# A two-layer MoE behind attention on one core: first layer's activation applied in place to batches of whole chunks, evictions as plain copies

## The chip, the cores and the metric

One core of a Trainium2 chip. The time is device microseconds of one execution of the whole program. The kernel before ran three times: median 517.15 us, 516.41 to 517.77 us.

## The reference

Local attention plus attention on a four-fold downsampled sequence, for 2 batches x 8 heads x 576 positions x 64; its result is x, 1152 tokens x 512. Then two layers of matmuls in float32 accuracy:

```python
h = x @ w_in                                   # 1152x512 @ 512x2048
sp = np.where(h > 20.0, h, np.log1p(np.exp(np.minimum(h, 20.0))))
g = h * np.tanh(sp)                            # Mish
x = g @ w_out                                  # 2048 -> 512
silu = (x @ w_gate) * sigmoid(x @ w_gate)      # 512 -> 1536
out = (silu * (x @ w_val)) @ w_out2            # 1536 -> 512
```

The weights come as 64-bit floats.

## The kernel before

**Work.** Everything stays on chip between the stages. Float32 accuracy is made from pairs: each operand is split into a rounded part (`hi`, a copy to another type) and the rest (`lo`, a subtraction), and three matmuls (`mm3`, lines 763 to 765) take the place of one. A weight strip of 128 x 512 is loaded as raw 64-bit words and rebuilt by `convert`: two ScalarE steps with the function Prelu (`fold`, line 286; `field`, line 290), a VectorE step (`join`, line 293), then `hi` (line 219 on ScalarE or 221 on VectorE) and `lo` (line 307).

**First layer.** `l1(f, i)` makes chunk f (128 of the 2048 hidden columns, 16 chunks) for piece i of the tokens (three pieces of 384): a group of 12 matmuls in two halves (`cols_group`) into one of seven PSUM banks. The bank is emptied into a third of the chunk's H buffer. For chunks 0 to 5 and pieces 0 and 1 that is a plain copy (`early`), since the attention still runs; in all other cases the activation Mish is applied on the way (line 803, ScalarE). `split` then applies Mish in place to the two copied pieces of chunks 0 to 5 (line 822), and splits the whole chunk of 1152 tokens into G (`hi`, line 219 or 221; `lo`, line 829). There are six H and six G buffers; chunk 6 takes the H buffer of chunk 0, and so on. `l2` multiplies G with the second weight, four chunks at a time, in twelve groups of 12 matmuls. The second layer (`l3`, `l4`) follows, with Silu on ScalarE.

**Order.** A planner (`Plan.run`) writes the order of every engine before anything is issued. Each step has the engines that may run it with a cost on each, its dependencies, the buffers that it takes, and a due time `want`; among the steps that could start, an engine takes the one with the least `want`. ScalarE's functions come in tables: a step may name a table, and when this is not the last one loaded, the planner adds 8.0 to its due time and 1.28 us to its cost. Mish names "mish", the exponentials of the attention "exp", Silu "silu"; `fold` and `field` name none. Where nothing is ready, PE gets a filler matmul (`warm`, line 1194, the first 95 us only), so that it is never idle for long. Each engine then works through its order and waits where an input is not there.

In the names of the rows: b is a PSUM bank, H a chunk, G its split, cw a weight under conversion, raw its bytes, wt its split, xy the tokens' split x, warm the filler's bank.

Of the kernel before, what the change touches and what calls it, by code (L numbers as in the profile page):

```python
# [22 lines left out]
NTOK = 1152  # L23
PC = 384
# [8 lines left out]


SLOPE = 2.0 ** -40


class Ring:
# [37 lines left out]
class Plan:  # L76
# [15 lines left out]
    def run(self):  # L92
        names = ["PE", "ACT", "DVE", "POOL", "SP"]
        free = dict.fromkeys(names, 0.0)
        ready = {e: [] for e in names}
        for n, o in enumerate(self.ops):
            o.n = n
            if not o.left:
                for e in o.eng:
                    ready[e].append(o)  # L100
        table, now, order = None, 0.0, []
        todo = len(self.ops)
        while todo:
            later, ran = [], False
            for e in names:
                if free[e] > now:
                    later.append(free[e])
                    continue
                best = None
                for o in ready[e]:  # L110
                    t = o.at
                    for r in o.rings:
                        t = max(t, r.free_at(sum(x.ring is r for x in o.new)))
                    if t > now:
                        later.append(t)
                        continue
                    w = o.want + (8.0 if o.table and o.table != table else 0.0)
                    if best is None or (w, o.n) < best[0]:
                        best = ((w, o.n), o)
                if best is None:  # L120
                    if e == "PE" and self.spare and self.spare[1] <= now < self.spare[2]:
                        free[e] = now + self.spare[3] * (2 if now < COLD else 1)
                        later.append(free[e])
                        order.append((now, self.spare[0], e))
                        ran = True
                    continue
                o = best[1]
                ran = True
                todo -= 1
                for f in o.eng:  # L130
                    ready[f].remove(o)
                for x in o.new:
                    x.ring.give(x)
                d = o.eng[e]
                if o.table and o.table != table:
                    d, table = d + self.TABLE, o.table
                free[e] = now + (d if e != "SP" else max(0.5, d))
                o.ran = e
                o.end = free[e] + (2.2 if e == "SP" else 0.0)
                later.append(free[e])  # L140
                order.append((now, o, e))
                for x in o.use:
                    x.left -= 1
                    x.free_at = max(x.free_at, o.end + self.REMOTE)
                for c in o.out:
                    c.left -= 1
                    same = e in c.eng and len(c.eng) == 1
                    c.at = max(c.at, free[e] if same and e in ("PE", "SP") else o.end + (self.LOCAL if same else self.REMOTE))
                    if not c.left:
                        for f in c.eng:  # L150
                            ready[f].append(c)
            if not ran:
                nxt = [t for t in later if now < t < 1e8]
                if not nxt:
                    raise RuntimeError("no order found: " + str([(o.fn.__qualname__.split(".")[-1], [next((t for t, r in self.rings.items() if r is x.ring), "?") for x in o.new], o.at) for e in names for o in ready[e]]))
                now = min(nxt)
        self.length = max(o.end for o in self.ops)
        for _, o, e in order:
            o.fn(e)
# [3 lines left out]
def attention_moe_kernel(  # L163
# [38 lines left out]
    def us_tt(n):  # L202
        return n / 960 + 0.069
# [4 lines left out]
    def us_act(n, psum=False):  # L208
        return n / 1200 + (0.051 if psum else 0.093)
# [48 lines left out]
    def convert(kind, f, want, lead=None):  # L258


        src = srcs[kind]
        wide = src.dtype != F32
        m = 8 if wide else 1
        src = src.bitcast(U8) if wide else src
        raw = buf(wp, [128, 4104 if wide else 512], U8 if wide else F32, "raw", RAWS)
        wt = buf(wp, [128, 2, 512], F32R, "wt", WTS)
        cw = buf(wp, [128, 512], F32, "cw", CWS) if wide else raw
        w0 = want - (lead or 10.33)

        def load(e):  # L270
            t = raw.make()
            t = t[:, 1:4097] if wide else t
            if kind in "1gv":
                nc.sync.dma_start(
                    out=t.rearrange("p (c f) -> p c f", c=4),
                    in_=src[:, 128 * m * f:128 * m * (f + 1)].rearrange("(c p) f -> p c f", p=128),
                )
            else:
                nc.sync.dma_start(out=t, in_=src[128 * f:128 * (f + 1), :])

        prev = conv_chain[0] or {}
        o_load = plan.add({E_SP: 1.46}, load, [prev.get("load")], w0 - 10.0, [raw])
        last = o_load
        if wide:
            def fold(e):
                ACT.activation(cw.make(), raw.tile[:, 8:4104].bitcast(I8).rearrange("p (n b) -> p n b", b=8)[:, :, 0],  # L286
                               AF.Prelu, scale=-1.0, bias=-56.0, alpha=SLOPE)

            def field(e):
                ACT.activation(cw.tile.bitcast(I32), cw.tile, AF.Prelu, scale=-2.0 ** 27 / SLOPE, bias=-112 * 2.0 ** 27, alpha=SLOPE)  # L290

            def join(e):
                DVE.scalar_tensor_tensor(out=cw.tile.bitcast(U32), in0=raw.tile[:, 0:4096].bitcast(U32).rearrange("p (n b) -> p n b", b=2)[:, :, 1],  # L293
                                         scalar=5, in1=cw.tile.bitcast(U32), op0=ALU.logical_shift_right, op1=ALU.bitwise_or)

            o_mag = o = plan.add({"ACT": us_act(512) + 0.1}, fold, [o_load, prev.get("mag")], w0, [cw], [raw])
            o = plan.add({"ACT": us_act(512)}, field, [o], w0, use=[cw])
            last = plan.add({"DVE": us_tt(512)}, join, [o], w0 + 1, use=[cw, raw])
        else:
            o_mag = None  # L300

        def hi(e):
            wt.make()
            copy(e, wt.tile[:, 0], cw.tile)

        def lo(e):
            DVE.tensor_tensor(out=wt.tile[:, 1], in0=cw.tile, in1=wt.tile[:, 0].bitcast(F32), op=ALU.subtract)  # L307

        o_hi = plan.add({"ACT": us_act(512), "DVE": us_ts(512)}, hi, [last, prev.get("hi")], w0 + 2, [wt], [cw])
        o_lo = plan.add({"DVE": us_tt(512)}, lo, [o_hi], w0 + 3, use=[wt, cw])  # L310
        conv_chain[0] = {"load": o_load, "mag": o_mag, "hi": o_hi}
        wts[kind, f], wt_ops[kind, f] = wt, o_lo
        return cw, last
# [473 lines left out]
    def l1(f, i, want):  # L787
# [6 lines left out]
        first = h.first is None  # L794
        ps, o, cs = cols_group("1", f, i, lambda: xt, xd + [h.first], want, [x_buf] + ([] if first else [h]), [h] if first else [])

        early = f < RING and i < 2

        def evac(e):
            if early:  # L800
                copy(e, h.tile[:, cs], ps.tile[:, 0:n])
            else:
                ACT.activation(h.tile[:, cs], ps.tile[:, 0:n], AF.Mish)  # L803

        if early:
            o = plan.add({"ACT": us_act(n, True), "DVE": us_tt(n)}, evac, [o], want - 4, use=[ps, h])
        else:
            o = plan.add({"ACT": us_act(n, True)}, evac, [o] + att_ops, want - 4, use=[ps, h], table="mish")
        if first:
            h.first = o  # L810
        h.ops.append(o)
        if i == 2:
            split(f, h, want)

    def split(f, h, want):

        add = plan.add
        g = G[f] = buf("g", GSHAPE, F32R, "G", 6)
        n = 2 * PC

        def mish(e):
            ACT.activation(h.tile[:, 0:n], h.tile[:, 0:n], AF.Mish)

        def hi(e):
            g.make()
            copy(e, g.tile[:, 0], h.tile)

        def lo(e):
            DVE.tensor_tensor(out=g.tile[:, 1], in0=h.tile, in1=g.tile[:, 0].bitcast(F32), op=ALU.subtract)

        if f < RING:
            h.ops.append(add({"ACT": us_act(n)}, mish, h.ops[:2] + att_ops, want - 2, use=[h], table="mish"))
        o = add({"ACT": us_act(NTOK), "DVE": us_ts(NTOK)}, hi, h.ops + att_ops, want + 4.0, [g], [h])
        G_ops[f] = add({"DVE": us_tt(NTOK)}, lo, [o], want + 4.0, use=[g, h])

    yacc = buf("acc", [128, 4, NTOK], F32, "acc", 1)
# [392 lines left out]
```

## Time and profile before

| | us |
|---|---|
| median of three runs | 517.15 |
| profiled execution, its own time | 517.0 |
| its span | 515.2 |
| PE busy | 494.1 |
| ACT busy | 339.0 |
| DVE busy | 323.2 |
| ACT table loads, 58 of 1283 ns | 74.4 |

PE is TensorE, ACT ScalarE, DVE VectorE. The time is 1.8 us above the span, which begins with the first and ends with the last recorded instruction. A busy share is a mean over stages; where an engine sets the pace is seen in the view by stretches and in the list of waits. A matmul's row lasts longer (some 0.34 us) than its distance to the next (0.17 us), since matmuls are pipelined.

### The profile page before, as it was taken

The page shows a single profiled execution, that of the slowest core. Times are in us where ns is not written, and L with a number is a line of the kernel's source. Part 1 is how long each engine was busy: PE and PEld are TensorE (multiplying, and loading weights), DVE is VectorE, ACT ScalarE, POOL GpSimd, SP SyncE. Part 2 cuts the span into 40 slices and gives each one's busy share as a digit, 9 for nine tenths or more (in the row PEclk, how much of TensorE's full clock was granted, in tenths as well). Part 3 has the DMA queues.
Part 4 walks back from the last instruction along what each step waited for, and adds up shares of the span by engine and source line. Part 5 has one row for each costly group of instructions (what it writes and reads, how often), then busy time and mean ns, then how long its engine had stood idle before and what let it go on. Part 6 is the DMA issues. An engine that isn't in the chain of part 4 may idle for free.

```text
span 515.2 us, 8535 instructions
## 1 busy us (share of the span) xinstructions
PE 494.1 (96%) x3315; PEld 459.3 (89%) x3315; DVE 323.2 (63%) x624; ACT 339.0 (66%) x681; POOL 23.9 (5%) x43
## 2 busy tenths in 40 slices
PE   9999999999669996999999999999999999999997
PEld 7777888999559986999999999999998899998885
DVE  3897999744421523563458899989886088882422
ACT  4889999899995999369925376655573276750000
POOL 4332210000000000000000000000000000000000
PEclk9999999999989999999999999999999999999999
DMA  9999734322231132212321113242254014320022
GB/s 175 194 159 219 183 108 133 124 83 81 71 91 44 42 122 83 83 41 83 122 83 42 41 41 124 83 122 83 82 164 124 0 42 123 93 72 1 0 91 93
DMA packets 58225, 48.23 MB, mean 94 GB/s; under 512 B 30664, under 2 KB 53448, under 8 KB 58184
## 3 DMA queue, kind: packets, MB, share of 16 engines
q1 hardware_dynamic: 58184, 47.68, 34.7%
q8 instruction: 26, 0.43, 0.4%
q14 instruction: 15, 0.12, 0.1%
HBM read 45.31 MB, written 2.36 MB: 93 GB/s over the span
## 4 chain that ended last, share of the span: by engine, by line
PE 75%; ACT 19%; issue 3%; DVE 2%; DMA 1%; ACTq 0%
PE b L763 17%; PE b L765 17%; PE b L764 17%; PE b L1051 5%; PE b L1053 5%; PE b L1052 5%; ACT L803 3%; PE warm L1194 2%; ACT L290 2%; ACT cw L286 2%; ACT L286 2%; ACT H L803 2%; PE b L643 2%; ACT cw L290 1%; PE b L698 1%
## 5 line engine op out<-in xcount | busy, mean ns | idle before, releaser
L763 PE MATMUL b<-xy,wt 128*128 128x384 f32 x384 | 129.9, 338 | 3.7 <-ACT H L803 3.7
L765 PE MATMUL b<-xy,wt 128*128 128x384 f32 x384 | 128.6, 335 | 0.0
L764 PE MATMUL b<-xy,wt 128*128 128x384 f32 x384 | 128.6, 335 | 0.0
L293 DVE SCALAR_TENSOR_TENSOR cw<-raw,cw 128x512 uint32<-128x512 uint32 x68 | 46.6, 687 | 64.3 <-ACT cw L290 64.2
L763 PE MATMUL b<-G,wt 128*128 128x384 f32 x192 | 66.2, 345 | 11.1 <-ACT H L803 10.5
L763 PEld LDWEIGHTS b<-xy,wt 128*128 128x128 f32 x384 | 72.1, 188 | 5.3 <-ACT H L803 4.7
L764 PEld LDWEIGHTS b<-xy,wt 128*128 128x128 f32 x384 | 72.1, 188 | 0.0
L765 PEld LDWEIGHTS b<-xy,wt 128*128 128x128 f32 x384 | 72.1, 188 | 0.0
L765 PE MATMUL b<-G,wt 128*128 128x384 f32 x192 | 65.1, 339 | 0.0
L764 PE MATMUL b<-G,wt 128*128 128x384 f32 x192 | 65.0, 338 | 0.0
L286 ACT ACTIVATE cw<-raw 128x512 f32<-128x512 int8 x68 | 45.7, 672 | 12.1 <-DVE wt L307 11.3
L219 ACT ACTIVATE G<-H 128x1152 fp32r<-128x1152 f32 x20 | 22.9, 1164 | 45.8 <-PE b L765 23.5
L307 DVE TENSOR_TENSOR wt<-cw,wt 128x512 fp32r<-128x512 f32 x68 | 46.7, 689 | 6.3 <-ACT wt L219 4.5
L763 PEld LDWEIGHTS b<-G,wt 128*128 128x128 f32 x192 | 36.5, 190 | 13.6 <-ACT H L803 12.8
L290 ACT ACTIVATE cw<-cw 128x512 int32<-128x512 f32 x68 | 43.0, 633 | 0.9
L1051 PE MATMUL b<-wt,G 128*128 128x512 f32 x108 | 42.3, 391 | 0.0
L1052 PE MATMUL b<-wt,G 128*128 128x512 f32 x108 | 42.2, 391 | 0.0
L1053 PE MATMUL b<-wt,G 128*128 128x512 f32 x108 | 42.2, 390 | 0.0
L764 PEld LDWEIGHTS b<-G,wt 128*128 128x128 f32 x192 | 36.5, 190 | 0.0
L765 PEld LDWEIGHTS b<-G,wt 128*128 128x128 f32 x192 | 36.5, 190 | 0.0
L221 DVE CAST wt<-cw 128x512 fp32r<-128x512 f32 x34 | 15.2, 446 | 32.6 <-PE b L1053 19.2
L219 ACT ACTIVATE H<-b 128x384 f32<-128x384 f32 x31 | 15.2, 489 | 27.4 <-PE b L765 27.3
(105 smaller groups left out, 845.9 us busy)
## 6 DMA issues: line engine op xcount, KB each, us to landing
raw<-in_moe_w_out_dram SPq DMA_DIRECT2D x28, 512.0 KB
raw<-in_moe_w_in_dram SPq DMA_DIRECT2D x16, 512.0 KB
raw<-in_moe_w_gate_dram SPq DMA_DIRECT2D x12, 512.0 KB
raw<-in_moe_w_val_dram SPq DMA_DIRECT2D x12, 512.0 KB
vw<-in_v_dram SPq DMA_DIRECT2D x36, 70.0 KB
vq<-in_v_dram SPq DMA_DIRECT2D x8, 288.0 KB
out_dram<-acc SPq DMA_DIRECT2D x9, 256.0 KB
qk<-in_q_dram SPq DMA_DIRECT2D x8, 256.0 KB
```

The lines of the kernel that those rows point to most:

```text
L219: ACT.activation(out, in_, AF.Copy)
L286: ACT.activation(cw.make(), raw.tile[:, 8:4104].bitcast(I8).rearrange("p (n b) -> p n b", b=8)[:, :, 0], AF.Prelu, scale=-1.0, bias=-56.0, ...
L290: ACT.activation(cw.tile.bitcast(I32), cw.tile, AF.Prelu, scale=-2.0 ** 27 / SLOPE, bias=-112 * 2.0 ** 27, alpha=SLOPE)
L293: DVE.scalar_tensor_tensor(out=cw.tile.bitcast(U32), in0=raw.tile[:, 0:4096].bitcast(U32).rearrange("p (n b) -> p n b", b=2)[:, :, 1], sca ...
L307: DVE.tensor_tensor(out=wt.tile[:, 1], in0=cw.tile, in1=wt.tile[:, 0].bitcast(F32), op=ALU.subtract)
L763: PE.matmul(out=ps, lhsT=wt_hi, rhs=m_hi, start=first, stop=False, **more)
L764: PE.matmul(out=ps, lhsT=wt_hi, rhs=m_lo, start=False, stop=False, **more)
L765: PE.matmul(out=ps, lhsT=wt_lo, rhs=m_hi, start=False, stop=last, **more)
L803: ACT.activation(h.tile[:, cs], ps.tile[:, 0:n], AF.Mish)
L1051: PE.matmul(out=ps.tile, lhsT=g[:, 0, tok], rhs=wt[:, 0], start=(f == fs[0]), stop=False)
L1052: PE.matmul(out=ps.tile, lhsT=g[:, 0, tok], rhs=wt[:, 1], start=False, stop=False)
L1053: PE.matmul(out=ps.tile, lhsT=g[:, 1, tok], rhs=wt[:, 0], start=False, stop=(f == fs[-1]))
```

## The change

Mish no longer rides on the eviction. Every piece of every chunk is copied out of PSUM plainly, by ScalarE or VectorE. When two chunks (for chunks 0 to 7) or four (8 to 11, 12 to 15) are there in full, one step applies Mish in place to all of them, 1152 elements at a time. The planner is told with `SERVED` which tables serve which step: the two Prelu steps of a conversion now name "sides", which the tables "exp" and "silu" serve and "mish" does not, so that they too cost a table load after a Mish. The due times of batch and splits are shifted, and `fold` is 0.05 cheaper for the planner.

```diff
+SERVED = {"exp": ("exp",), "mish": ("mish",), "silu": ("silu",), "sides": ("exp", "silu")}
...
-                    w = o.want + (8.0 if o.table and o.table != table else 0.0)
+                    w = o.want + (8.0 if o.table and table not in SERVED[o.table] else 0.0)
...
-                if o.table and o.table != table:
-                    d, table = d + self.TABLE, o.table
+                if o.table and table not in SERVED[o.table]:
+                    d, table = d + self.TABLE, SERVED[o.table][0]
...
-            o_mag = o = plan.add({"ACT": us_act(512) + 0.1}, fold, [o_load, prev.get("mag")], w0, [cw], [raw])
-            o = plan.add({"ACT": us_act(512)}, field, [o], w0, use=[cw])
+            o_mag = o = plan.add({"ACT": us_act(512) + 0.05}, fold, [o_load, prev.get("mag")], w0, [cw], [raw], "sides")
+            o = plan.add({"ACT": us_act(512)}, field, [o], w0, use=[cw], table="sides")
...
-        early = f < RING and i < 2
-
         def evac(e):
-            if early:
-                copy(e, h.tile[:, cs], ps.tile[:, 0:n])
-            else:
-                ACT.activation(h.tile[:, cs], ps.tile[:, 0:n], AF.Mish)
-
-        if early:
-            o = plan.add({"ACT": us_act(n, True), "DVE": us_tt(n)}, evac, [o], want - 4, use=[ps, h])
-        else:
-            o = plan.add({"ACT": us_act(n, True)}, evac, [o] + att_ops, want - 4, use=[ps, h], table="mish")
+            copy(e, h.tile[:, cs], ps.tile[:, 0:n])
+
+        o = plan.add({"ACT": us_act(n, True), "DVE": us_tt(n)}, evac, [o], want - 4, use=[ps, h])
...
-        def mish(e):
-            ACT.activation(h.tile[:, 0:n], h.tile[:, 0:n], AF.Mish)
+        def act(e):
+            ACT.activation(h.tile, h.tile, AF.Mish)
...
-        if f < RING:
-            h.ops.append(add({"ACT": us_act(n)}, mish, h.ops[:2] + att_ops, want - 2, use=[h], table="mish"))
-        o = add({"ACT": us_act(NTOK), "DVE": us_ts(NTOK)}, hi, h.ops + att_ops, want + 4.0, [g], [h])
-        G_ops[f] = add({"DVE": us_tt(NTOK)}, lo, [o], want + 4.0, use=[g, h])
+        batch.append((f, h, g, want, act, hi, lo))
+        if len(batch) < sizes[0]:
+            return
+        sizes.pop(0)
+        now = list(batch)
+
+        def all_(e):
+            for b in now:
+                b[4](e)
+
+        o = add({"ACT": len(now) * us_act(NTOK)}, all_, [o for b in now for o in b[1].ops] + att_ops, want + 1.8, use=[b[1] for b in now], table="mish")
+        for f, h, g, want, act, hi, lo in now:
+            x = add({"ACT": us_act(NTOK), "DVE": us_ts(NTOK)}, hi, [o], want + 7.96, [g], [h])
+            G_ops[f] = add({"DVE": us_tt(NTOK)}, lo, [x], want + 7.96, use=[g, h])
+        batch.clear()
+
+    batch, sizes = [], list((2, 2, 2, 2, 4, 4))
```

The diff moves lines by 3 to 6 and changes the planner's order on every engine. ScalarE's queue shortly after the attention, while chunks 0 to 3 are activated; before (L803 and L822 are Mish, L286 and L290 the conversion):

```order
L803 ACT_TABLE_LOAD
L803 ACTIVATE H_1110<-b_159 128x384
L290 ACT_TABLE_LOAD
L290 ACTIVATE cw_1065<-cw_1065 128x512
L219 ACTIVATE G_1603<-H_1110 128x1152
L803 ACT_TABLE_LOAD
L803 ACTIVATE H_1210<-b_179 128x384
L286 ACT_TABLE_LOAD
L286 ACTIVATE cw_892<-raw_814 128x512
L803 ACT_TABLE_LOAD
```

and changed (L816 is Mish, L289 and L293 the conversion, L222 a copy):

```order
L816 ACT_TABLE_LOAD
L816 ACTIVATE H_1079<-H_1079 128x1152
L816 ACTIVATE H_1164<-H_1164 128x1152
L289 ACT_TABLE_LOAD
L289 ACTIVATE cw_892<-raw_814 128x512
L222 ACTIVATE H_1299<-b_209 128x384
L222 ACTIVATE wt_1242<-cw_1111 128x512
L816 ACT_TABLE_LOAD
L816 ACTIVATE H_1230<-H_1230 128x1152
L816 ACTIVATE H_1299<-H_1299 128x1152
L293 ACT_TABLE_LOAD
```

Ten rows held five loads; now eleven hold four, and between the two batches the conversion and the evictions follow each other without one. In the whole queue 58 loads have become 14.

VectorE's queue at the same place, up to the subtractions that give the H buffers of chunks 0 and 1 back; before (H_983 and H_1110 are the two chunks, L829 the subtraction):

```order
L221 CAST G_1583<-H_983 128x1152
L293 SCALAR_TENSOR_TENSOR cw_979<-raw_1006,cw_979 128x512
L829 TENSOR_TENSOR G_1583<-H_983,G_1583 128x1152
L221 CAST wt_1034<-cw_892 128x512
L293 SCALAR_TENSOR_TENSOR cw_1065<-raw_897,cw_1065 128x512
L829 TENSOR_TENSOR G_1603<-H_1110,G_1603 128x1152
```

and changed (H_1079 and H_1164 are the two chunks, H_1230 and H_1299 chunks 2 and 3, L823 the subtraction):

```order
L224 COPY H_1230<-b_229 128x384
L224 CAST wt_1162<-cw_987 128x512
L310 TENSOR_TENSOR wt_1162<-cw_987,wt_1162 128x512
L224 COPY H_1299<-b_179 128x384
L224 CAST G_1650<-H_1079 128x1152
L224 CAST G_1658<-H_1164 128x1152
L823 TENSOR_TENSOR G_1650<-H_1079,G_1650 128x1152
L823 TENSOR_TENSOR G_1658<-H_1164,G_1658 128x1152
```

The first subtraction now stands behind both casts and behind the evictions of chunks 2 and 3 (their last pieces). On PE chunk 6, which takes chunk 0's H buffer, comes after the last pieces of chunks 0 to 3 and the middle pieces of chunks 3 and 4.

PE's queue in the attention, where a score step of the second batch is followed by the first work of the first layer; before (L638 and L643 are a score step, L763 the first matmul of chunk 0):

```order
L638 LDWEIGHTS identb
L638 MATMUL b_209<-masks,identb 128x210
L643 MATMUL b_209<-qkT_158 64x70 x6
L763 MATMUL b_159<-xy_82,wt_930 128x384
L764 MATMUL b_159<-xy_82,wt_930 128x384
```

and changed (L641 and L646 are a score step, L1200 the filler):

```order
L641 LDWEIGHTS identb
L641 MATMUL b_195<-masks,identb 128x210
L646 MATMUL b_195<-qkT_228 64x70 x6
L1200 LDWEIGHTS wsrc
L1200 MATMUL warm<-wsrc 128x256
```

The last two rows stand there 15 times before the next step; chunk 0 begins later. In the whole queue 103 fillers have become 113, and the last step of the attention comes after 17 half groups of the first layer where it came after 15.

## Rows read from the trace of the kernel before

**Rows 1.** The page: busy time of the engines, and PE and ACT in 40 slices.

```profile
PE 494.1 (96%) x3315; PEld 459.3 (89%) x3315; DVE 323.2 (63%) x624; ACT 339.0 (66%) x681; POOL 23.9 (5%) x43
...
PE   9999999999669996999999999999999999999997
...
ACT  4889999899995999369925376655573276750000
```

**Rows 2.** Busy time by stretches of the span, all engines, granted clock, DMA.

```profile
core 0: us, PE busy (x) PEld busy (x) DVE busy (x) ACT busy (x) POOL busy (x), PEclk, DMA share, GB/s
40.00:93.00 53.00, 53.00 (x678) 43.88 (x680) 47.62 (x133) 50.12 (x199) 8.12 (x9) 1.00 0.63 151
124.00:155.00 31.00, 21.60 (x108) 19.46 (x107) 11.49 (x16) 30.48 (x36) 0.00 (x0) 0.94 0.25 80
146.00:148.00 2.00, 2.00 (x8) 2.00 (x7) 0.00 (x0) 1.97 (x3) 0.00 (x0) 0.50 0.42 172
155.00:184.00 29.00, 29.00 (x168) 29.00 (x167) 9.60 (x14) 22.86 (x34) 0.00 (x0) 1.00 0.23 71
184.00:208.00 24.00, 18.57 (x103) 17.28 (x102) 8.24 (x12) 23.63 (x28) 0.00 (x0) 1.00 0.22 69
208.00:500.00 292.00, 292.00 (x1593) 280.97 (x1592) 199.13 (x349) 155.01 (x250) 0.00 (x0) 1.00 0.25 76
```

**Rows 3.** PE's waits: line waited for, us in total, times, longest.

```profile
PE b L763 <- ACT H L803: 14.2, 8, 4.1
```

**Rows 4.** PE's timeline at seven places: start, length, instruction, idle time before it.

```profile
93.21 0.44 PE L763 MATMUL b<-xy,wt 128*128 128x384 f32 x1
...
94.37 0.35 PE L763 MATMUL b<-xy,wt 128*128 128x384 f32 x1
...
125.68 0.45 PE L763 MATMUL b<-G,wt 128*128 128x384 f32 x1
...
145.62 0.52 PE L764 MATMUL b<-G,wt 128*128 128x384 f32 x1
145.94 0.52 PE L765 MATMUL b<-G,wt 128*128 128x384 f32 x1
...
167.55 0.33 PE L763 MATMUL b<-xy,wt 128*128 128x384 f32 x1
...
224.33 0.34 PE L763 MATMUL b<-xy,wt 128*128 128x384 f32 x1
...
299.61 0.34 PE L763 MATMUL b<-xy,wt 128*128 128x384 f32 x1
```

**Rows 5.** ACT's timeline: an eviction in the first layer, and one alternation of tables.

```profile
94.57 0.49 ACT L219 ACTIVATE H<-b 128x384 f32<-128x384 f32 x1 [1.37 <-PE b L765]
...
109.95 0.66 ACT L286 ACTIVATE cw<-raw 128x512 f32<-128x512 int8 x1
110.63 1.28 ACT L803 ACT_TABLE_LOAD   x1
111.92 0.49 ACT L803 ACTIVATE H<-b 128x384 f32<-128x384 f32 x1
```

**Rows 6.** ACT's groups by line: busy us, mean ns of one, idle time before.

```profile
L803 ACT ACT_TABLE_LOAD x23 | 29.5, 1283 | 0.4
L219 ACT ACTIVATE G<-H 128x1152 fp32r<-128x1152 f32 x20 | 22.9, 1164 | 45.8 <-PE b L765 23.5 <-PE b L1052 21.8
L822 ACT ACTIVATE H<-H 128x768 f32<-128x768 f32 x6 | 5.0, 842 | 0.1
```

**Rows 7.** DVE's groups by line and shape.

```profile
L829 DVE TENSOR_TENSOR G<-H,G 128x1152 fp32r<-128x1152 f32 x16 | 21.4, 1354 | 10.7 <-ACT G L219 10.7
L221 DVE COPY H<-b 128x384 f32<-128x384 f32 x17 | 9.4, 555 | 6.3 <-PE b L765 6.2
L221 DVE CAST G<-H 128x1152 fp32r<-128x1152 f32 x8 | 6.0, 756 | 4.0 <-ACT H L803 3.5 <-PE b L1052 0.4
```

**Rows 8.** The chain of waits, near the start: start, us, what (fillers).

```profile
5.23 1.09 PE warm L1194 x10
```

More of the change, by code (lines that the diff above doesn't have):

```diff
@@ L812, in l1, with mish @@
         if i == 2:
-            split(f, h, want)
-    def split(f, h, want):
+            mish(f, h, want)
+    def mish(f, h, want):
         add = plan.add
         g = G[f] = buf("g", GSHAPE, F32R, "G", 6)
-        n = 2 * PC
-        def mish(e):
-            ACT.activation(h.tile[:, 0:n], h.tile[:, 0:n], AF.Mish)
+        def act(e):
+            ACT.activation(h.tile, h.tile, AF.Mish)
         def hi(e):
```

## The prediction

> **What bounds the kernel now.** I read the page first. TensorE (PE) is busy for 494.1 us of a span of 515.2 us and ScalarE (ACT) for 339.0 us, so over the whole span PE is the limit; but PE's row of 40 slices has one dent, 9 9 6 6 9 9 6 9 from about 142 to 206 us, and ACT's row stands at 9 through the same slices [rows 1]. The table by stretches puts numbers on it: from 40 to 93 us, the attention, PE is busy all the time; from 124 to 155 us for 21.60 us of 31 with ACT at 30.48; from 155 to 184 us all the time with ACT at 22.86; from 184 to 208 us for 18.57 us of 24 with ACT at 23.63; and from 208 to 500 us all the time again [rows 2]. So ACT sets the pace in two stretches, both in the first MoE layer, and PE everywhere else. The list of PE's waits agrees: 14.2 us in 8 waits, all for ACT's line 803, the Mish activation that empties a PSUM bank [rows 3].
>
> That list understates the loss, because the end of a matmul is modelled. I therefore count matmuls between places of the program that can be recognized by their start [rows 4]. From 224.33 us (first matmul of chunk 12) to 299.61 us (second MoE layer) PE never waits: 36 groups of 12 matmuls, 432 in 75.28 us, 0.1743 us each. The same price applied further up: 93.21 to 125.68 us holds 31 half groups, 186 matmuls, 32.4 us; it took 32.47, nothing lost. 125.68 to 167.55 us (first product with G to chunk 8) holds 168, 29.3 us; it took 41.87, **12.6 us lost**. 167.55 to 224.33 us holds 24 groups, 288, 50.2 us; it took 56.78, **6.6 us lost**. Together 19.2 us. The 5.0 us above the listed 14.2 are what a wait costs around itself: the modelled end hides some 0.16 us of each, the first step after a pause is about 0.3 us instead of 0.17, and after the longest wait (4.1 us) the matmuls stand 0.32 us apart for a while, with a granted clock of 0.50, the 1.2 GHz level [rows 2 to 4].
>
> Why is ACT late? Its timeline alternates: conversion, table load, one Mish eviction, table load, conversion [rows 5]. Each load takes 1.283 us against 0.49 us for the eviction that it serves [rows 5, 6]. There are 58 loads in the program, 74 us of ACT.
>
> **The change, part by part.**
>
> *Loads.* The changed order has 14 table loads: one for the exponentials, six pairs around the six batches of Mish, one for Silu. 44 loads go, 44 x 1.283 = 56.5 us of ACT. All 44 stood in the first layer, where 56 of the 58 were: of every four loads there three go. ACT was full there, and PE waited for it, in two stretches of 55 us together; PE lost 19.2 us, a third of what ACT is freed of. So ACT stops being the limit, and what follows as limit is PE itself, at 0.1743 us per matmul. I therefore book the whole loss: **-19.2 us**, and no more, since where PE does not wait a lighter ACT is worth nothing.
>
> *Evictions and activations.* 48 evictions become plain copies that DVE may also take, and 16 whole-chunk activations are added; DVE gets 10 evictions more than before, and 7 splits of G move from ACT to DVE: 10 x 0.555 + 7 x 0.756 = 10.8 us [rows 7]. DVE was busy for 11.49 us of 31 and 8.24 of 24 in the two stretches [rows 2], so this is covered. A whole-chunk Mish is priced at 1.16 us, as the copy of the same shape (Mish on 768 elements took 0.842) [rows 6]. Later, from 208 us on, order and work are almost the same; cost nothing.
>
> *Latency at the first reuse of an H buffer.* This is the new wait that could come. There are six H buffers, chunk 6 takes that of chunk 0, and its first matmul waits for DVE's second split of chunk 0, which waits for the batch of chunks 0 and 1. From the end of the last group of chunk 1, PE has four groups to do before it: 4 x 12 x 0.1743 = 8.4 us. ACT's side: an eviction starts 0.2 us after PE begins the next group (94.37 to 94.57) [rows 4, 5], 0.555 for DVE's copy [rows 7], 1.28 for the load, 2 x 1.16: done 4.4 us after the group's end. DVE's side: in its queue stands, ahead of the two casts, the eviction of chunk 3, whose group PE ends 4.2 us after; plus 0.2 and 0.555 that is 4.9; two casts of 0.756 and a subtraction of 1.354 make 7.8 [rows 7], 0.2 for the signal makes 8.0. Against 8.4 it just fits, with 0.4 us to spare. The later batches have longer covers: those of chunks 8 to 11 and 12 to 15 are followed by a whole block of twelve second-matmul groups, 25 us. Only where the second matmul turns to chunk 14 does its split stand close to its use again, behind the split of two weights on DVE; at worst one subtraction, 1.354 us, is late there. I take **+0.4 us** for all of it, between 0 and 3.
>
> The first rows on this price: a load begins at 110.63 us right as the activation before it ends (109.95 + 0.66), and the next activation starts at 111.92, 1.29 us after the load's start [rows 5]; nothing is lost besides. The Trainium skill ("ScalarE: Activation LUTs", What ACT_TABLE_LOAD costs) says otherwise: about 1283 ns for the load and about 1380 ns more for a drain, 2.66 us for each switch. By that price, an estimate, ACT's side above would end near 5.8 us instead of 4.4, DVE's casts would start 0.9 us later, and PE would wait about half a microsecond at this place, so that the sum would be near 499.8 us. The trace contradicts the drain, and the sum keeps 1.28.
>
> *The attention part.* The planner's new order is not the old one there either. Up to the last step of attention ACT has one more conversion and two more splits of x and one eviction less, PE two half groups more (they are done early, and missing later) and 10 more filler matmuls, 113 against 103. PE was busy throughout from 40 to 93 us [rows 2], so a filler there is on the path: ten took 1.09 us [rows 8]. **+1.1 us**, with 0 as the other end, if PE would have waited at these places.
>
> *Sum*, against the profiled execution (517.0 us, span 515.2): 517.0 - 19.2 + 0.4 + 1.1 = **499.3 us**. The profiled execution is 0.15 us under the median of the three runs, 517.15, so against that the change is worth 3.4%. From here on I call 0.3% (1.5 us) the least that a measurement of this kernel tells from no change.
>
> **The rivals.**
>
> *Waits return at the reuse of buffers (chance 0.18).* The spare 0.4 us is less than one DVE instruction. If one more of them (0.7 to 1.35 us) [rows 7] stands in front, or a weight comes late, chunk 6 waits, and something like it can happen at each of the six batches. For it: the thin margin, and that the planner's own costs, not the chip's, made the order. Against: the five other batches have covers of 10 us and more. Price 1 to 6 us: 500.5 to 505.
>
> *Attention turns from PE-bound to ACT-bound (0.12).* ACT was busy for 50.12 us of 53 there [rows 2], and has about 1.8 us more to do (two conversion steps of 0.66 and two copies less one of 0.49) [rows 5]; DVE gets two evictions and a conversion step for two splits. Against: the part also grows by 3.2 us of PE work, the half groups and the fillers. Price 1 to 4 us: 500.5 to 503.5.
>
> *The batches block the evictions (0.03), slower than before.* A batch of two holds ACT for 2 x 1.283 + 2 x 1.16 = 4.9 us, one of four for 7.2. If everything that PE waits for queued behind, the six batches would cost 4 x 4.9 + 2 x 7.2 = 34 us: 517.0 - 19.2 + 1.1 + 34 = 533 us. It decides once more than 53% of that reaches PE. Against it: seven PSUM banks of 2.09 us each give PE 14.6 us before a late eviction stops it, and after the batches of four DVE evicts.
>
> *The loads stay (0.01):* then 517 to 518. The loads are instructions of the program, and 14 of them stand in the changed one.
>
> **How the numbers follow.** The forecast, 497.8 to 500.5, has 0.66; its lower end is the whole loss back with nothing added. The range of **496.5 to 506.0** takes in the forecast and both milder rivals. Faster by over 0.3%: 0.95; within: 0.02; slower: 0.03.
>
> **What would show it.** Right: 14 table loads; no wait of PE for ACT above half a microsecond after 93 us; PE's slices at 9 without a dent; 168 and 288 matmuls between the same marks in 29.3 and 50.2 us; ACT's slices in the dent well under 9. Chunk 6's first matmul, the first with a buffer that the batch gives back, is the place to look for a wait for DVE's subtraction. Wrong: a stretch of PE waits before 95 us, or any wait for an activation of 1152 elements. If the loss vanished and the span were still above 502, the attention part took it.

## The result, and the profile after

The changed kernel took **498.94 us** (median of 4 runs, 498.15 to 499.6) beside 516.85 us (4 runs, 516.41 to 517.77): 0.9651 of the time, 95% interval 0.9629 to 0.9672. The forecast was 499.3 us, the range 496.5 to 506.0. The profiled execution took 498.15 us, its span 496.4.

The page of the changed kernel, busy time and slices of 12.4 us, to be held against [rows 1]:

```profile
PE 490.6 (99%) x3325; PEld 459.1 (92%) x3325; DVE 331.6 (67%) x640; ACT 284.2 (57%) x631; POOL 23.5 (5%) x43
...
PE   9999999999999999999999999999999999999996
...
ACT  4889999688936553455342765656672385730000
```

PE's dent is gone. From 136 to 211 us ACT's slices stand at 3 to 6; before, where PE's slices showed a 6, they stood at 9. The same stretches as in [rows 2] (length, PE, weight loads, DVE, ACT, POOL busy, granted clock, DMA share, GB/s):

```profile
40.00:93.00 53.00, 52.89 (x661) 44.16 (x656) 45.98 (x131) 50.12 (x195) 7.61 (x9) 1.00 0.69 171
124.00:155.00 31.00, 31.00 (x179) 31.00 (x178) 11.70 (x19) 19.44 (x27) 0.00 (x0) 1.00 0.21 72
155.00:184.00 29.00, 29.00 (x168) 29.00 (x168) 15.17 (x24) 17.74 (x31) 0.00 (x0) 1.00 0.41 127
184.00:208.00 24.00, 24.00 (x138) 24.00 (x138) 13.63 (x20) 10.03 (x13) 0.00 (x0) 1.00 0.07 23
```

PE is busy in all of them, at the full clock. All of PE's waits that are left lie before 93 us; the line with 14.2 us [rows 3] has no successor:

```profile
PE warm L1200 <- DVE wsrc L386: 1.2, 1, 1.2
PE b L466 <- DVE xs L711: 0.4, 1, 0.4
PE b L569 <- ACT ed L558: 0.2, 1, 0.2
```

PE's timeline at the places of [rows 4], and at chunk 6 (111.08):

```profile
95.31 0.45 PE L766 MATMUL b<-xy,wt 128*128 128x384 f32 x1
...
111.08 0.33 PE L766 MATMUL b<-xy,wt 128*128 128x384 f32 x1
...
125.64 0.34 PE L766 MATMUL b<-G,wt 128*128 128x384 f32 x1
...
155.16 0.33 PE L766 MATMUL b<-xy,wt 128*128 128x384 f32 x1
...
205.48 0.33 PE L766 MATMUL b<-xy,wt 128*128 128x384 f32 x1
...
280.76 0.34 PE L766 MATMUL b<-xy,wt 128*128 128x384 f32 x1
```

Between the same marks:

| stretch | before, us | after, us | difference |
|---|---|---|---|
| start to end of the attention | 93.21 | 95.31 | +2.10 |
| to the first product with G | 32.47 | 30.33 | -2.14 |
| to chunk 8 (168 matmuls) | 41.87 | 29.52 | -12.35 |
| to chunk 12 (288) | 56.78 | 50.32 | -6.46 |
| to the second layer (432) | 75.28 | 75.28 | 0.00 |
| to the end of the span | 215.6 | 215.6 | 0.0 |

The first two lines cancel: two half groups (12 matmuls at 0.1743 us, 2.09 us of PE work) moved from behind the mark to ahead of it. In the traces 13 half groups stand ahead of it before and 15 after; the text ahead of the prediction counts 15 and 17, with the same difference. What is left is the loss of the two stretches, 18.8 us, and it has come back.

ACT's groups by line (busy us, mean ns of one, idle before), for [rows 6]:

```profile
L222 ACT ACTIVATE H<-b 128x384 f32<-128x384 f32 x56 | 27.4, 489 | 50.0 <-PE b L768 49.5
L816 ACT ACTIVATE H<-H 128x1152 f32<-128x1152 f32 x16 | 17.6, 1157 | 0.1
L816 ACT ACT_TABLE_LOAD x6 | 7.7, 1283 | 0.1
```

Six loads for Mish where there were 28 (23 and 5 for its two lines), 14 in all for 58. A Mish of a whole chunk takes 1157 ns, forecast at 1.16 us. The evictions on ACT now wait 49.5 us for PE.

### The profile page after: what moved, and what is told of

The parts are those of the page before. It is cut to its first block, busy times and chain, and to the rows that moved or that the text cites. A ratio compares the mean times of both kernels' runs of the same rounds, so it can differ in the third digit from the quotient of the medians.

```text
span 496.4 us, 8519 instructions
## 1 busy us (share of the span) xinstructions
PE 490.6 (99%) x3325; PEld 459.1 (92%) x3325; DVE 331.6 (67%) x640; ACT 284.2 (57%) x631; POOL 23.5 (5%) x43
## 3 DMA queue, kind: packets, MB, share of 16 engines
q1 hardware_dynamic: 58184, 47.68, 35.5%
## 4 chain that ended last, share of the span: by engine, by line
PE 92%; ACT 5%; DVE 2%; issue 0%; ACTq 0%
PE b L766 23%; PE b L768 23%; PE b L767 23%; PE b L1057 5%; PE b L1059 5%; PE b L1058 5%; PE b L701 2%; PE warm L1200 2%; PE b L646 1%; ACT ex L660 1%; PE b L686 1%; ACT ed L545 1%; PE b L466 1%; ACT qkT L483 1%; PE b L530 1%; PE b L581 1%
## 5 line engine op out<-in xcount | busy, mean ns | idle before, releaser
L766 PE MATMUL b<-G,wt 128*128 128x384 f32 x192 | 64.8, 337 | 0.0
L768 PE MATMUL b<-G,wt 128*128 128x384 f32 x192 | 64.7, 337 | 0.0
L767 PE MATMUL b<-G,wt 128*128 128x384 f32 x192 | 64.4, 335 | 0.0
L222 ACT ACTIVATE H<-b 128x384 f32<-128x384 f32 x56 | 27.4, 489 | 50.0 <-PE b L768 49.5
L289 ACT ACTIVATE cw<-raw 128x512 f32<-128x512 int8 x68 | 45.4, 668 | 14.4 <-DVE wt L310 12.7
L310 DVE TENSOR_TENSOR wt<-cw,wt 128x512 fp32r<-128x512 f32 x68 | 46.2, 684 | 3.9 <-ACT wt L222 2.1
L224 DVE CAST wt<-cw 128x512 fp32r<-128x512 f32 x31 | 13.1, 423 | 50.9 <-PE b L767 31.7
L293 ACT ACTIVATE cw<-cw 128x512 int32<-128x512 f32 x68 | 42.8, 629 | 1.2
L222 ACT ACTIVATE G<-H 128x1152 fp32r<-128x1152 f32 x13 | 14.7, 1164 | 49.9 <-PE b L768 27.8
L767 PEld LDWEIGHTS b<-G,wt 128*128 128x128 f32 x192 | 36.0, 188 | 0.0
L766 PEld LDWEIGHTS b<-G,wt 128*128 128x128 f32 x192 | 36.0, 188 | 0.0
L768 PEld LDWEIGHTS b<-G,wt 128*128 128x128 f32 x192 | 36.0, 188 | 0.0
```

Of the source, the lines that this page charges most:

```text
L222: ACT.activation(out, in_, AF.Copy)
L224: DVE.tensor_copy(out=out, in_=in_)
L766: PE.matmul(out=ps, lhsT=wt_hi, rhs=m_hi, start=first, stop=False, **more)
L767: PE.matmul(out=ps, lhsT=wt_hi, rhs=m_lo, start=False, stop=False, **more)
L768: PE.matmul(out=ps, lhsT=wt_lo, rhs=m_hi, start=False, stop=last, **more)
```

## The experiments

Every ratio is to the kernel before on the same chip, with its 95% interval. "Loads" are table loads in the trace.

| run | what | loads | us, median | ratio |
|---|---|---|---|---|
| the change | | 14 | 498.94 | 0.9651 (0.9629 to 0.9672) |
| e1_loads_half | change, loads put back at every second late conversion | 28 | 498.51 | 0.9643 (0.9628 to 0.9658) |
| e2_loads_back | at all late conversions | 48 | 505.33 | 0.9774 (0.9757 to 0.9791) |
| e3_loads_more | twice in each of them | 84 | 551.09 | one run |
| e4_loads_ctrl | as e2, with a function that needs no load | 14 | 498.2 | 0.9635 (0.9617 to 0.9653) |
| e5_served_only | before, with the account of loads alone | 48 | 499.03 | 0.9657 (0.9637 to 0.9678) |
| e6_batch_unserved | change without the account | 14 | 498.5 | 0.964 (0.9614 to 0.9665) |
| e7_sizes1 | batches of one chunk | 30 | 498.77 | 0.9653 (0.9635 to 0.967) |
| e8_sizes4 | batches of four | 10 | 498.67 | 0.9652 (0.9627 to 0.9677) |
| e9_after_nolate | change, last 31 of 113 fillers left out | 14 | 499.66 | 0.968 (0.9655 to 0.9705) |
| e10_before_nolate | before, last 21 of 103 fillers left out | 58 | 519.6 | 1.0059 (1.0038 to 1.0079) |
| e11_before_copies | before, its order kept, conversions' Prelu replaced by copies | 3 | 498.27 | 0.9644 (0.9624 to 0.9665) |
| e12_served_58 | e5, with loads put back | 58 | 498.53 | 0.9651 (0.9627 to 0.9675) |

### Loads put back into the changed order

The order of the changed kernel is kept. A Mish on one column of a tile that nobody reads stands ahead of `fold` in the 20 conversions that run late (first weight from chunk 8 on, second weight from strip 4 on), so that the Prelu behind it has to load its table again.

```diff
+                if kind == "1" and f >= 8 or kind == "2" and f >= 4:
+                    ACT.activation(dum, dum, AF.Mish)
                 ACT.activation(cw.make(), raw.tile[:, 8:4104].bitcast(I8).rearrange("p (n b) -> p n b", b=8)[:, :, 0],
```

This is e2. In e1 the condition has `and f % 2 == 0` besides; in e3 the same two lines stand ahead of `field` too; in e4 the function is Copy.

e1_loads_half:

> The changed kernel with its order untouched; ahead of the first Prelu step of every second conversion of chunks 8 to 15 and of second-weight strips 4 to 15 stands one Mish on a single column, which forces 14 table loads back (28 instead of 14). Theory (the loads filled ScalarE): 14 x 1.283 = 18 us of ScalarE more, where it was busy for 69.8 of 115 us (93 to 208 us of the changed kernel's span): still slack, so 498.5 to 500.5 us. Rival (the gain came from plain copies, of which VectorE takes a share, or from the new order): no dependence on loads at all, 498.9 us here and in the two kernels with more loads.

e2_loads_back:

> The same Mish on one column ahead of the first Prelu step of all 20 conversions: 34 loads back, 48 in the program. Theory: 34 x 1.283 = 43.6 us on top of 69.8 of 115 us fill ScalarE in that stretch, and TensorE's waits for evictions and activations come back in part: 502 to 512 us. Rival (copies and order are what counts): 498.9 us.

e3_loads_more:

> The Mish on one column ahead of both Prelu steps of these 20 conversions: 70 loads back, 84 in the program. Theory: 70 x 1.283 = 90 us and 40 small activations of about 0.2 us, 8 us, on top of some 78 us that ScalarE works between 95 and 225 us: 176 us of work in 130 us, so ScalarE sets the pace and the program ends some 45 us later, 535 to 550 us. Rival (copies and order): 498.9 us.

e4_loads_ctrl:

> Control: at the 20 places of the kernel with 34 loads back a plain Copy on one column in place of the Mish, 14 loads as in the changed kernel. Theory and rival alike: 20 x about 0.2 us of ScalarE, 498.5 to 499.8 us. If this one is slower by more than 1 us, the inserted step itself costs, not the load.

Measured: e1 nothing (its interval overlaps that of the change), e2 +6.4 us, e3 +52 us in its single run, a little above what was expected, and the control e4 nothing (498.2 us, 0.3 below its range), so it is the loads and not the 20 instructions. In this order the first 14 loads put back cost nothing; the next 20, 25.7 us of ACT, cost 6.8 us; the last 36, 46.2 us of ACT, with 20 more of the small Mish, cost 45.8 us. So loads cost little until ACT is full, and then nearly all that they last. The stretch from 124 to 155 us and PE's waits for evictions, in e2 and then in e3:

```profile
124.00:155.00 31.00, 29.00 (x157) 28.68 (x156) 12.60 (x19) 30.62 (x43) 0.00 (x0) 0.94 0.26 82
...
PE b L770 <- ACT H L222: 4.0, 3, 2.0
```

```profile
124.00:155.00 31.00, 20.93 (x108) 19.98 (x106) 9.07 (x13) 30.57 (x39) 0.00 (x0) 0.94 0.18 51
...
PE b L772 <- ACT H L222: 30.8, 8, 6.2
PE b L772 <- DVE H L224: 5.5, 2, 3.8
```

The waits are of the kind seen before, PE behind a late eviction on ACT, though that eviction is a plain copy (L222) here. ACT's timeline of e2 shows what it stands behind: two conversion steps, an added Mish with its load, and the load back:

```profile
141.67 1.28 ACT L290 ACT_TABLE_LOAD   x1
142.97 0.20 ACT L290 ACTIVATE dum<-dum 128x1 f32<-128x1 f32 x1
143.19 1.28 ACT L291 ACT_TABLE_LOAD   x1
144.48 0.65 ACT L291 ACTIVATE cw<-raw 128x512 f32<-128x512 int8 x1
145.16 0.63 ACT L295 ACTIVATE cw<-cw 128x512 int32<-128x512 f32 x1
145.70 0.47 ACT L222 ACTIVATE H<-b 128x384 f32<-128x384 f32 x1
```

PE's next group begins at 146.22 us, after 2.00 us of waiting for that copy. In e3 DVE's evictions come late as well.

### The two halves of the change, each alone

e5 is the kernel before with the `SERVED` lines, the table "sides" on `fold` and `field`, and the 0.05 (the first four hunks of the diff); Mish rides on the evictions as before. e6 is the changed kernel without the last of these hunks:

```diff
-            o_mag = o = plan.add({"ACT": us_act(512) + 0.05}, fold, [o_load, prev.get("mag")], w0, [cw], [raw], "sides")
-            o = plan.add({"ACT": us_act(512)}, field, [o], w0, use=[cw], table="sides")
+            o_mag = o = plan.add({"ACT": us_act(512) + 0.1}, fold, [o_load, prev.get("mag")], w0, [cw], [raw])
+            o = plan.add({"ACT": us_act(512)}, field, [o], w0, use=[cw])
```

e5_served_only:

> The kernel before with the planner's new account of tables alone: the two Prelu steps name the tables that serve them, Mish stays on the eviction. 48 loads instead of 58. Theory (the batches take the loads away, the account does little): 10 x 1.283 = 12.8 us of ScalarE less where it is full, so part of the 19.2 us back: 505 to 514 us. Rival (the account is the change: the planner no longer takes an order for cheap that is not): 499 to 502 us.

e6_batch_unserved:

> The changed kernel without the account: the two Prelu steps name no table and the first has its old cost, batches and plain copies stay. The program has 14 loads all the same. Theory (batches do it): 498 to 501 us. Rival (the account): above 505 us.

Measured: each half alone gives the whole gain, 499.03 and 498.5 us. e6 is what the theory said. **e5 is not**: 48 loads remain, and PE never waits for them; the theory, by which the loads themselves cost the time, was wrong, and the rival, by which the account is enough, right. In e5 ACT is busy nearly throughout from 155 to 184 us, and PE too:

```profile
155.00:184.00 29.00, 29.00 (x169) 29.00 (x168) 17.43 (x25) 28.62 (x38) 0.00 (x0) 1.00 0.28 91
```

So the number of loads does not decide alone. Two kernels with 48 loads, e2 and e5, are 6.3 us apart. e6 keeps batches and plain copies together; which of the two suffices without the account was not tried.

### The size of a batch

```diff
-    batch, sizes = [], list((2, 2, 2, 2, 4, 4))
+    batch, sizes = [], list((1,) * 16)
```

This is e7; e8 has `(4, 4, 4, 4)`.

e7_sizes1:

> The changed kernel with 16 batches of one chunk: 30 loads. Theory: 16 x 1.283 = 20.5 us more of ScalarE, covered as ScalarE has some 45 us of slack between 93 and 208 us; the first split comes earlier than with batches of two: 498 to 501 us. Rival (the size of the batch matters by itself): above 504 us.

e8_sizes4:

> The changed kernel with four batches of four chunks: 10 loads. Theory (loads no longer matter, and the first reuse of an H buffer is the tight place): the batch of chunks 0 to 3 ends two groups and 2.2 us of Mish later than that of chunks 0 and 1, so chunk 6 comes later in TensorE's order or TensorE waits for VectorE's subtraction, 0 to 4 us: 499 to 503 us. Rival (fewer loads are always better): 497.5 to 498.5 us.

Measured: 498.77 and 498.67 us, no difference. e7 is what the theory said; e8 lies between the two ranges of its expectation, and its four runs (497.6 to 499.86) reach into both, so it decides for neither. With 30 loads ACT has 26.63 us of work in 155 to 184 us, still under the 29; with 10 it has 17.76. From 97 us on PE waits for nothing in either. In e8 the planner itself put the first product with G earlier (120.42 us), so the long latency of a batch of four was not put to the test at its hardest place.

### The fillers

The last term of the prediction's sum booked ten more fillers at 1.1 us. In e9 and e10 all fillers behind the 82nd are not issued:

```diff
+            count[0] += 1
+            if count[0] > 82:
+                return
```

e9_after_nolate:

> The changed kernel in its own order, with the last 31 of its 113 filler matmuls not issued (those after the 82nd, all in the second half of the attention). If fillers there lie on the path, as the prediction booked them: 31 x 0.109 = 3.4 us less, 495.5 us. If they stand where TensorE would wait for ScalarE or VectorE anyway: 498.9 us, and the trace shows some 3.4 us of waits in their place. If the clock falls without them: slower than 499.

e10_before_nolate:

> The kernel before in its own order, with the last 21 of its 103 fillers not issued (those after the 82nd). Fillers on the path: 21 x 0.109 = 2.3 us less, 514.6 us. Fillers in waits: 516.9 us, with some 2.3 us of waits in their place.

Measured: leaving them out gains nothing. The changed kernel was the same (499.66 us, 6 runs from 498.71 to 503.61), the kernel before became **slower**, 0.59% (0.38 to 0.79%). In both traces PE waits where fillers had stood, and the granted clock falls after it. Before, from 60 to 70 us:

```profile
60.00:65.00 5.00, 5.00 (x61) 4.24 (x60) 4.57 (x16) 4.37 (x19) 0.00 (x0) 1.00 0.75 147
65.00:70.00 5.00, 5.00 (x70) 4.15 (x68) 4.32 (x12) 5.00 (x21) 2.45 (x3) 1.00 0.52 144
```

and e10:

```profile
60.00:65.00 5.00, 4.34 (x41) 3.39 (x41) 4.34 (x14) 5.00 (x23) 0.00 (x0) 0.76 0.98 208
65.00:70.00 5.00, 5.00 (x34) 4.02 (x33) 2.19 (x8) 2.56 (x11) 2.75 (x3) 0.56 0.39 111
```

PE had 41 matmuls for 61 in the first five microseconds, most of the missing ones fillers, it was idle for 0.66 us, and the granted clock fell; in the second, at 0.56, near the 1.2 GHz level, it had 34 for 70, while ACT and DVE were busy for half of it. In e9 the waits are longer:

```profile
55.00:60.00 5.00, 2.56 (x39) 1.93 (x36) 4.72 (x17) 5.00 (x23) 0.46 (x1) 0.94 0.89 229
60.00:65.00 5.00, 5.00 (x54) 4.57 (x52) 3.40 (x9) 4.47 (x20) 0.73 (x1) 0.72 0.98 208
```

PE was idle for 2.44 us of the first of these, in which 25 of the 31 fillers had stood and the changed kernel had PE busy throughout. So of e9's three expectations the second, fillers in waits, is borne out for the most part, and the third, the clock, in part. What waits and clock cost each was not separated. In e10 the attention ends at 94.44 us, 1.23 later, and the stretch after it takes 33.79 us instead of 32.47. Its granted clock there is 1.00, and PE's list of the whole execution has one wait for Mish more than before (9 in 15.4 us). Why ACT is that much later there was not followed up.

### Before's own order, without the loads

e11 keeps the order of the kernel before on every engine and replaces the two Prelu of a conversion by copies of the same shapes. In the rebuilt weights sign and exponent are then constants.

```diff
-                               AF.Prelu, scale=-1.0, bias=-56.0, alpha=SLOPE)
+                               AF.Copy, scale=0.0)
...
-                ACT.activation(cw.tile.bitcast(I32), cw.tile, AF.Prelu, scale=-2.0 ** 27 / SLOPE, bias=-112 * 2.0 ** 27, alpha=SLOPE)
+                ACT.activation(cw.tile.bitcast(I32), cw.tile, AF.Copy, scale=0.0, bias=1006632960.0)
```

> The kernel before, order untouched on every engine, with both Prelu steps of a conversion replaced by Copy of the same shapes, a function that needs no table: 3 loads in place of 58. (The weights' sign and exponent are a constant in this kernel; their mantissa is still joined.) Theory (the loads alone made ScalarE late, the order of before is good if they cost nothing, as its planner believed): all 19.2 us come back, 497 to 499.5 us. Rival (the order of before is bad in itself: conversions ahead of evictions): part of the loss stays, 503 us or more.

Measured: 498.27 us. The two steps themselves last as long as before (671 and 630 ns for 672 and 633), so only the loads went. Three loads are left, for the exponentials, Mish and Silu, which are the three that before's planner counted. The order of before was good for a program with three loads; what ran had 58. The stretch from 124 to 155 us:

```profile
124.00:155.00 31.00, 31.00 (x178) 31.00 (x177) 5.12 (x10) 10.87 (x21) 0.00 (x0) 1.00 0.21 69
```

### 58 loads in an order that counts them

e12 has the order of e5 and puts ten loads back, by the one-column Mish ahead of `fold` in five conversions, to reach the 58 of before:

```diff
+                if (kind, f) in (("1", 11), ("2", 5), ("2", 6), ("2", 9), ("2", 10)):
+                    ACT.activation(dum, dum, AF.Mish)
```

> The kernel with the account alone (48 loads, 499.0 us), order untouched, with a Mish on one column ahead of five conversions' first step (chunk 11, second-weight strips 5, 6, 9 and 10), all of them after the last product of the first two chunks of the layer has begun or later: ten loads more, 58 as in the kernel before, and 12 instead of 6 in the stretch of the first block of second matmuls, as there. If the number of loads is what counts: 505 to 517 us. If it counts where they stand in ScalarE's order against what TensorE waits for: 498 to 501 us.

Measured: 498.53 us, where before took 516 to 517 with as many loads. Their number does not decide; where they stand, and what else ACT has to do there, does. The stretch from the first product with G to chunk 8 shows it. For before, here are the stretch ahead of it, itself (from 125.68 us) and the one behind it, then ACT's groups in it that differ most:

```profile
93.21:125.68 32.47, 32.47 (x190) 32.27 (x186) 14.65 (x22) 30.03 (x36) 0.00 (x0) 1.00 0.33 112
125.68:167.55 41.87, 32.47 (x169) 30.54 (x169) 13.24 (x21) 35.53 (x47) 0.00 (x0) 0.96 0.21 63
167.55:224.33 56.78, 51.34 (x289) 50.06 (x289) 23.46 (x38) 44.50 (x54) 0.00 (x0) 1.00 0.25 75
...
L219 ACT ACTIVATE acc<-b 128x384 f32<-128x384 f32 x11 | 4.9, 497 | 5.8 <-PE b L765 5.8
L803 ACT ACTIVATE H<-b 128x384 f32<-128x384 f32 x6 | 2.8, 487 | 0.0
L822 ACT ACTIVATE H<-H 128x768 f32<-128x768 f32 x2 | 1.7, 843 | 0.0
```

and for e12 the stretch ahead, from the end of the attention, and the same matmuls (from 126.17 us):

```profile
95.83:126.17 30.34, 30.34 (x179) 30.34 (x176) 20.77 (x30) 28.19 (x33) 0.00 (x0) 1.00 0.17 54
126.17:155.69 29.52, 29.52 (x170) 29.52 (x170) 11.48 (x20) 29.07 (x40) 0.00 (x0) 1.00 0.34 101
...
L222 ACT ACTIVATE acc<-b 128x384 f32<-128x384 f32 x7 | 2.9, 496 | 0.0
L810 ACT ACTIVATE H<-b 128x384 f32<-128x384 f32 x4 | 1.9, 490 | 0.0
```

Counted over all of ACT's groups, both hold 13 loads, 16.7 us. But before gave ACT 35.53 us of work for a stretch that PE does in 29.5, and in between ACT stood idle for 5.8 us ahead of evictions of acc (the sum of the products with G), waiting for PE; at other moments PE waited for ACT. Of the 12.35 us lost, 6.0 are this excess of work and 6.3 are ACT's idle time. In e12 ACT needs 29.07 of 29.52 us, with four evictions of acc, two Mish evictions and two Mish in place fewer, and PE runs through. DVE has taken over part ahead of it, with 20.77 us of work where it had 14.65. Which of the moved steps matters most was not tried one by one.

The second stretch of before needs a finer cut. From 167.55 to 224.33 us ACT had 44.50 us of work in all, less than the 50.3 that PE needs, and 6.5 us were lost all the same. They were lost where ACT was full within it: from 184 to 208 us ACT worked for 23.63 us [rows 2], while PE's 103 matmuls, at 0.1743 us, need 18.0.

No version beat the changed kernel by more than the intervals: all those with their fillers in which PE does not wait stand between 498.2 and 499.0 us. The two halves don't add, since both end at PE.

## Why the prediction was right, point by point

**What bounds it.** Right. PE was held by ACT in two stretches, and at PE's own pace everywhere else; freed, they took 29.52 and 50.32 us, as said (29.3 and 50.2). The 40 slices were misread: PE's row has its 6s in slices 11, 12 and 16 (129 to 155 and 193 to 206 us), with three 9s between them and not two, and ACT's row has a 5 between them. The table by stretches and the marks, on which the sum rests, were read rightly.

**Loads, -19.2 us.** The mechanism is shown: e11 removes the loads alone and gains all; e2 puts 34 back and loses a third of it again, e3 puts 70 back and loses more than it. The size is -18.8. The uniform 0.1743 us per matmul was a little low for the first of the two stretches: its 168 took 29.52 us, 0.1757 each, without a wait in the change, e11 and e12 alike. The step that needs a correction is the reason given, "So ACT stops being the limit" because 44 loads go. It is true of this change, but more than was needed: e1 with 28 loads, e5 with 48 and e12 with 58 lose nothing. The fault of before was an order made for three loads, and each half of the change mends it, by making the loads few or by counting them. The text took the account for a detail of the order and gave it no term; alone it is worth the same 18 us.

**Evictions and activations at nothing.** Right: DVE's 331.6 us are 8.4 more than before (10.8 were booked), and PE waits for none of it. Of the 48 evictions only 36 changed, since 12 were plain copies before; DVE has 11 more such copies than before (10 were booked).

**The first reuse of an H buffer, +0.4 us.** The mechanism ran as written, with no wait. ACT's and DVE's timelines around the first batch:

```profile
103.83 1.28 ACT L816 ACT_TABLE_LOAD   x1
105.12 2.22 ACT L816 ACTIVATE H<-H 128x1152 f32<-128x1152 f32 x2
107.36 1.28 ACT L289 ACT_TABLE_LOAD   x1
```

```profile
107.12 0.56 DVE L224 COPY H<-b 128x384 f32<-128x384 f32 x1 [0.46 <-PE b L768]
107.59 1.42 DVE L224 CAST G<-H 128x1152 fp32r<-128x1152 f32 x2
108.93 1.35 DVE L823 TENSOR_TENSOR G<-H,G 128x1152 fp32r<-128x1152 f32 x1
```

The first subtraction ends at 108.93 + 1.35 = 110.28 us, chunk 6 begins at 111.08: 0.8 us to spare, or 0.6 with the 0.2 us that the prediction adds for the signal; 0.4 were forecast. The two Mish take 2.22 us, not 2.32, and the casts 1.42, not 1.51. The term measured 0.

Beside it stood the price of a load. The load starts at 103.83 and lasts 1.28, the next activation starts at 105.12: nothing besides, as in [rows 5]. By the Trainium skill ("ScalarE: Activation LUTs", What ACT_TABLE_LOAD costs) some 1.4 us of drain would come on top. The traces do not agree: in all fourteen the next activation starts 11 or 12 ns behind every load but the program's first, where the activation waits for PE. The waiting that the drain would have caused did not come.

**The attention part, +1.1 us.** In the profiled pair the mark moved by 2.10 us, of which the two half groups are 2.09: for the fillers nothing is left. Single profiles differ by as much as the term, though: with 103 fillers and 13 half groups the mark stands at 93.21, 93.63 and 93.87 us (before, e11, e6), with 113 and 15 between 95.31 and 96.89, mean 95.90 (the change, e1 to e5, e7, e8, e12). Less the half groups the means are 0.2 us apart, so 1.1 is not borne out, and a cost of some tenths is not excluded. e6 shows besides that this part belongs to the account and not to the batches: without the account there are 103 fillers and 13 half groups. That a filler costs its time because "PE was busy throughout" was the weak argument: e9 and e10 take fillers out and gain nothing, since PE waits at their places and the clock falls. For the waits the prediction had left room, with 0 as the other end.

**The rivals.** Waits at the reuse of buffers: none. Attention bound by ACT: 50.12 us of 53 as before, no wait above 0.4 but the first filler's at the start. Batches that block evictions: no wait for a Mish of 1152 elements, and e8 with four batches of four has none either. The loads went.

In the profiled pair the sum came out 1.1 us high, 499.3 for 498.15: the loss was 0.4 smaller, and the two costs, 0.4 and 1.1, did not show. The errors of loss and costs pull opposite ways, so part of the closeness is luck; the mechanism and its large term do not rest on it.

## What to carry to other kernels

Where an engine looks full beside one that waits, count what it needs between two marks of the program against what the waiting engine needs there: 35.5 us against 29.5 is a bound, 29.1 is not, and both read as "busy all the time". The marks must stand close: over the whole second stretch 44.5 against 50.3 us looked harmless, and 23.6 against 18.0 within it was the bound. A planner that does not count a cost makes an order that is right for another program; counting it can be worth as much as removing it, and where both cures end at the same engine they do not add. Filler matmuls in a mixed phase can look like work on the path: here leaving them out gained nothing in one kernel and cost 0.59% in the other.

## What the runs showed of the hardware that was not expected

- The fillers' worth. Without 21 of them the granted clock was 0.76 and 0.56 over ten microseconds that had 1.00 before, and the program was 0.59% slower. Neither expectation of e10 named it.
- ACT busy for 30.5 us of 31 without any wait of PE, in e12, where the same reading [rows 2] went with 9.4 us of idle PE:

```profile
124.00:155.00 31.00, 31.00 (x179) 31.00 (x178) 12.18 (x20) 30.52 (x42) 0.00 (x0) 1.00 0.30 89
```

- Waits of PE and a lower clock, together in one place and not in another: in e3, with waits of up to 6.2 us, the granted clock was 0.94, 0.88 and 0.83 in the three stretches from 124 to 208 us; before, from 184 to 208 us, PE stood idle for 5.4 us in four waits of at most 1.6 us, and the clock stayed at 1.00 [rows 2].
